# A decode-attention kernel's last projection: two half-width strips, five weight loads, and an unevenly dealt last load

## The chip, the cores and the metric

The kernel runs on one core of one Trainium2 chip. The metric is the device time of one execution in microseconds (us), as the median of several runs. The time of a run is about 2 us longer than the span of its profile (before: 1331.99 for the profiled run, span 1329.9). Times inside an execution are us from the start of the profile's span.

In the views, PE is the matrix engine, PEld its weight loads, DVE the vector engine, ACT the scalar engine and SPq the queue of the sync engine. SBUF is the on-chip memory, and PSUM the one in which matmuls add up. A column strip is a part of PE's columns on which a matmul is placed. A load is split over up to 16 DMA queues (the traces record 16 landings for a load of 128 rows), and its landing is the moment at which one of them, or the last, reports its share as done. The traces don't name the queue of a packet or of a landing. The PE clock is the share of the full clock that was granted.

## The reference

Two attention layers decode one token each. A has 32 heads over 32768 keys. B has 32 query heads over 8 key heads and looks at the last 4096 keys only. Each ends with a projection of its 4096 values to 512.

```python
def _A_ref(x, k_cache, v_cache, wq, wo):            # B: same, with 8 kv heads and a window of 4096 keys
    q = (x @ wq).reshape(B, Sq, H, Dh).transpose(0, 2, 1, 3)
    p = softmax(einsum("bhqd,bhkd->bhqk", q, k_cache) * Dh ** -0.5)
    o = einsum("bhqk,bhkd->bhqd", p, v_cache)
    return o.transpose(0, 2, 1, 3).reshape(B, Sq, H * Dh) @ wo      # wo: 4096 x 512
out = concatenate([a, b], axis=-1)                                  # 1 x 1 x 1024
```

## The kernel before

The kernel streams 570 MB of keys, values and weights through SBUF. A's weights `wo` come last. They lie in SBUF as 128 rows of 32 blocks; a block is 128 x 512 values (128 KB), and one matmul per block adds its part to one PSUM row of 512. The four loads are all issued long ahead, on one queue of the sync engine, and each has a semaphore of its own.

```python
WO_CUTS = {"A": (0, 12, 22, 28, 32), "B": (0, 16, 32)}

def load_wo(self, name, part):
    a0, a1 = self.WO_CUTS[name][part:part + 2]
    src = self.X[name]["wo"].rearrange("(p a) c -> p (a c)", a=32)
    ...
    self.load(self.kbuf[:, off + 512 * a0:off + 512 * a1], src[:, 512 * a0:512 * a1],
              self.wosem[name][part], self.free["k"][t])

def proj_part(self, name, part, out):
    ...
        for a in range(a0, a1):
            row, pos, begin, end = out(a)
            inst = e.matmul(row, lhsT=oz[:, a:a + 1], rhs=wo[:, 512 * a:512 * a + 512], start=begin, stop=end,
                            tile_position=pos, skip_group_check=True)
    return self.op("pe", mm, (self.wosem[name][part], 16), self.c[name]["ozop"])

def store(self, name, bank, off, dep):
    o = self.op("dve", lambda v: v.tensor_copy(self.out_sb[0:1, off:off + 512], bank[0:1, :]), dep)
    self.op("sp", lambda e: e.dma_start(self.out[0, :, off:off + 512], self.out_sb[0:1, off:off + 512])
            .then_inc(self.outsem[name], 16), o)

def emit_proj(self):
    ...                                          # B's 32 matmuls, in four column strips; copy to pb
    for part in range(len(self.WO_CUTS["A"]) - 1):
        last = self.proj_part("A", part, lambda a: (self.PT[0:1, :], None, a == 0, a == 31))
        if part == 0:
            o = ...                              # the matmul that sums B's four strips
            self.store("B", self.ACC, 512, o)
    self.store("A", self.PT, 0, last)
```

## Time and profile before

Part 2 of the page of the kernel before, the two DMA lines: the share in which the 16 DMA engines are busy, in tenths, and GB/s, in 40 slices of the span.

```profile
DMA  9999999999999999999999999999999999999997
GB/s 391 432 432 435 437 428 432 436 438 430 432 434 434 436 432 434 430 440 432 434 430 440 432 432 430 442 430 434 430 440 432 432 432 440 432 432 432 433 435 306
```

The loads bind everywhere but in the last slice. So only the end can change. The chain of waits of the kernel before, its last pieces: start, length, and what the kernel waited for.

```profile
1289.88 28.05 DMA kbuf<-in_A_wo_dram
1317.93 0.04 issue
1317.98 4.41 PE psPT L649 x12
1322.39 0.89 PE psACC L667 x2
1323.27 4.33 PE psPT L649 x20
...
1327.63 0.68 DVE out_sb L655
```

PE waits for A's first 12 blocks, and then it is PE that takes the time: 9.6 us of matmuls, although the last weights land at 1324.09. The view of waits of the kernel before (us in total, times, longest) says the same: one wait for A's weights.

```profile
PEld psPT L649 <- DMA kbuf<-in_A_wo_dram: 3.2, 1, 3.2
```

The windows view of the kernel before. Its last three columns are what is needed here: granted PE clock, share in which the DMA engines are busy, GB/s.

```profile
core 0: us, PE busy (x) PEld busy (x) DVE busy (x) ACT busy (x) POOL busy (x), PEclk, DMA share, GB/s
1318.00:1320.00 2.00, 2.00 (x7) 0.65 (x8) 0.00 (x0) 0.00 (x0) 0.00 (x0) 0.73 0.99 401
1320.00:1321.00 1.00, 1.00 (x4) 0.36 (x3) 0.00 (x0) 0.00 (x0) 0.00 (x0) 0.50 0.75 307
```

PE has half its clock in part of this time. Between 1320 and 1321 a quarter of the DMA engines' time is idle, since some have finished; those that work move 307 / (0.75 x 16) = 25.6 GB/s each.

The trace also records when each of the 16 queues of a load reports its share as landed. For A's last load in the kernel before:

```
1320.77 1320.87 1320.90 1321.01 1321.11 1321.48 1321.48 1321.90 1322.07 1322.10 1322.24 1322.24 | 1323.75 1323.97 1324.05 1324.09
```

Twelve queues finish 1.5 to 3.3 us ahead of the last four. The trace has twelve instruction fetches of 16 KB, 1.0 to 1.1 us each. After the one at 1318.06 a fourth queue joined three late ones, set back by 1.2 to 1.6 (which of the four it is isn't recorded); and four are late in the landings of each of the three loads that follow. What made the other three late isn't shown.

### The profile page before, as it was taken

How to read it: one execution, taken by the hardware profiler on the slowest of the kernel's cores; microseconds unless marked ns; L12 is line 12 of the kernel's file. 1: busy time of each engine (PE TensorE's matmuls, PEld its weight loads, DVE VectorE, ACT ScalarE, POOL GpSimd, SP SyncE). 2: the span in 40 equal slices, each digit the busy share in tenths (PEclk: the TensorE clock that was granted, in tenths of full speed). 3: DMA queues.
4: the chain of work that ended last, by engine and by line, in shares of the span. 5: the costliest groups of instructions: out<-in, count | busy, mean ns of one | idle time of the engine just before them, and what ended most of it. 6: DMA issues, size and time to landing. Idle time of an engine off the chain costs nothing.

```text
span 1329.9 us, 28729 instructions
## 1 busy us (share of the span) xinstructions
PE 970.0 (73%) x13402; PEld 682.1 (51%) x13402; DVE 751.7 (57%) x1345; ACT 54.8 (4%) x167; POOL 2.3 (0%) x17
## 2 busy tenths in 40 slices
PE   3756678687677878767787876778777776877786
PEld 3544456554445655444465544446554444655552
DVE  3654466655556666554566655456665545666562
ACT  0000000000000000000000000000000000000000
POOL 0000000000000000000000000000000000000000
PEclk9767898878879887887988788798878779888888
DMA  9999999999999999999999999999999999999997
GB/s 391 432 432 435 437 428 432 436 438 430 432 434 434 436 432 434 430 440 432 434 430 440 432 432 430 442 430 434 430 440 432 432 432 440 432 432 432 433 435 306
DMA packets 12931, 570.66 MB, mean 429 GB/s; under 512 B 1522, under 2 KB 1524, under 8 KB 1780
## 3 DMA queue, kind: packets, MB, share of 16 engines
q1 hardware_dynamic: 12628, 570.43, 99.3%
q8 instruction: 12, 0.20, 0.1%
q10 hardware_dynamic: 288, 0.00, 0.0%
q14 instruction: 3, 0.02, 0.0%
HBM read 570.43 MB, written 0.00 MB: 429 GB/s over the span
## 4 chain that ended last, share of the span: by engine, by line
DMA 69%; PE 28%; DVE 2%; issue 0%; ACT 0%; SPq 0%
DMA kbuf<-in_A_k_cache_dram 64%; PE psT L491 24%; PE psS L513 4%; DMA kbuf<-in_B_k_cache_dram 3%; DMA kbuf<-in_A_wo_dram 2%; DVE kt L494 1%; PE psPT L649 1%; PE psACC L593 0%; SPq L286 0%; DVE oc_A L609 0%; PE psACC L667 0%; PE psPT L565 0%; ACT psb L541 0%; DVE tr_in L530 0%; DVE out_sb L655 0%
## 5 line engine op out<-in xcount | busy, mean ns | idle before, releaser
L494 DVE COPY kt<-psT 128x1024 bf16<-128x1024 bf16 x1056 | 656.5, 685 | 245.4 <-PE psT L491 243.8
L491 PE MATMUL psT<-ident,kbuf 128*128 128x128 bf16 x8448 | 582.9, 235 | 174.1 <-DMA kbuf<-in_A_k_cache_dram 162.1
L491 PEld LDWEIGHTS psT<-ident,kbuf 128*128 128x128 bf16 x8448 | 543.5, 107 | 266.5 <-DMA kbuf<-in_A_k_cache_dram 170.2
L593 PE MATMUL psACC<-vbuf,ptsb 128*4 128x512 bf16 (+1 forms) x2112 | 181.0, 517 | 22.8 <-ACT ptsb L568 22.0
L513 PE MATMUL psS<-kt,qw 128*32 128x512 bf16 x2048 | 157.6, 385 | 15.5 <-DVE kt L494 15.5
L607 DVE TENSOR_SCALAR oc_A<-psACC,hot_A 128x128 f32<-128x128 f32 x32 | 11.2, 351 | 245.0 <-PE psG L620 245.0
L593 PEld LDWEIGHTS psACC<-vbuf,ptsb 128*4 128x4 bf16 (+1 forms) x2112 | 58.6, 109 | 135.3 <-issue 84.9
L541 ACT ACTIVATE psb<-psS,nb_A 128x512 bf16<-128x512 f32 x32 | 22.0, 687 | 1170.0 <-DVE nb_A L540 1170.0
L513 PEld LDWEIGHTS psS<-kt,qw 128*32 128x32 bf16 x2048 | 34.0, 95 | 58.0 <-DVE kt L494 31.4
L620 PE MATMUL psG<-oc_A,hw 128*32 128x128 f32 (+1 forms) x128 | 19.3, 227 | 52.3 <-DVE oc_A L609 52.3
L620 PEld LDWEIGHTS psG<-oc_A,hw 128*32 128x32 f32 x128 | 11.4, 109 | 62.5 <-DVE oc_A L609 55.0
L565 PE MATMUL psPT<-ident,psb 128*128 128x128 bf16 x136 | 17.4, 268 | 34.0 <-ACT psb L541 34.0
L609 DVE SCALAR_TENSOR_TENSOR oc_A<-psACC,hot_A,oc_A 128x128 f32<-128x128 f32 x96 | 33.7, 351 | 3.4
L530 DVE TENSOR_REDUCE tr_in<-psS 128x1 f32<-128x512 f32 x34 | 23.5, 692 | 17.6 <-PE psS L513 17.6
L565 PEld LDWEIGHTS psPT<-ident,psb 128*128 128x128 bf16 x136 | 9.8, 114 | 37.1 <-ACT psb L541 36.7
L534 PE MATMUL psACC<-rows,tr_in 128*1 128x64 f32 x64 | 8.7, 217 | 25.5 <-DVE tr_in L530 25.5
L568 ACT ACTIVATE ptsb<-psPT 128x512 bf16<-128x512 bf16 x34 | 20.3, 597 | 28.9 <-PE psPT L565 28.9
L534 PEld LDWEIGHTS psACC<-rows,tr_in 128*1 128x1 f32 x64 | 2.7, 81 | 35.1 <-DVE tr_in L530 35.1
L538 PE MATMUL psACC<-mr_A,nscale 1*128 1x1 f32 x64 | 12.1, 256 | 9.7 <-DVE mr_A L537 9.7
L538 PEld LDWEIGHTS psACC<-mr_A,nscale 1*128 1x128 f32 x64 | 9.4, 182 | 15.7 <-DVE mr_A L537 15.7
L540 DVE COPY nb_A<-psACC 128x1 f32<-128x1 f32 x32 | 5.1, 158 | 15.0 <-PE psACC L538 15.0
L447 PE MATMUL psACC<-x_B,vbuf 128*128 128x1 bf16 x128 | 3.6, 165 | 13.6 <-DMA x_B<-in_B_x_dram 13.6
(71 smaller groups left out, 83.8 us busy)
## 6 DMA issues: line engine op xcount, KB each, us to landing
kbuf<-in_B_k_cache_dram SPq DMA_DIRECT2D x2, 4096.0 KB, 32.8
vbuf<-in_B_v_cache_dram SPq DMA_DIRECT2D x2, 4096.0 KB, 24.1
kbuf<-in_A_k_cache_dram SPq DMA_DIRECT2D x2, 4096.0 KB, 22.7
vbuf<-in_B_wq_dram SPq DMA_DIRECT2D x1, 4096.0 KB, 12.5
vbuf<-in_A_wq_dram SPq DMA_DIRECT2D x1, 4096.0 KB, 32.7
kbuf<-in_B_wo_dram SPq DMA_DIRECT2D x2, 2048.0 KB, 32.3
kbuf<-in_A_wo_dram SPq DMA_DIRECT2D x1, 1536.0 KB, 28.1
kbuf<-in_A_wo_dram SPq DMA_DIRECT2D x1, 1280.0 KB, 30.8
```

Source lines behind the costliest of these rows:

```text
L491: inst = e.transpose(T[:, 128 * k:128 * k + 128], src[:, DH * k:DH * k + DH], self.ident[:, :])
L494: self.copies.append(self.op("dve", lambda v: v.tensor_copy(KT[:, :], T[:, :]), o, to="pe"))
L513: inst = e.matmul(self.S[32 * c:32 * c + 32, :], lhsT=win, rhs=self.kt[(bb + c // 2) % NKT][:, 512 * (c % 2):512 * (c % 2) + 512], start=b ...
L530: o = dve(lambda v: v.reduce_max(tr["in"][:, 0:1], self.S[:, :], axis=AXX), self.sdone, self.k_pool, to="pe" if name == "A" else None)
L538: o = self.op("pe", lambda e: e.matmul(self.ACC[:, 64:65], lhsT=self.nscale[:, :], rhs=t["mr"][0:1, :], start=True, stop=True, skip_group_ ...
L541: self.sread = self.op("act", lambda s: s.activation(out=self.psb[:, :], in_=self.S[:, :], func=ACTF.Exp, bias=t["nb"][:, k:k + 1], scale= ...
L565: inst = e.transpose(PT[:, 128 * jj:128 * jj + 128], self.psb[:, 128 * jj:128 * jj + 128], self.ident[:, :])
L568: self.ptread = self.op("act", lambda s: s.activation(out=self.ptsb[:, :], in_=PT[:, 0:512], func=ACTF.Copy), self.psread, to="pe")
L593: inst = e.matmul(acc[32 * c:32 * c + rows, 0:512], lhsT=lhsT, rhs=rhs, start=begin, stop=end, tile_position=(0, 32 * c), skip_group_check ...
L609: o = self.op("dve", lambda v, src=src, hot=hot: v.scalar_tensor_tensor(out=oc, in0=src, scalar=hot, in1=oc, op0=ALU.mult, op1=ALU.add), p ...
L620: return self.op("pe", lambda e: e.matmul(self.G[0:32, c0 + c:c0 + c2], lhsT=win, rhs=t["oc"][g % 2][:, c:c2], start=False, stop=True, ski ...
L649: inst = e.matmul(row, lhsT=oz[:, a:a + 1], rhs=wo[:, 512 * a:512 * a + 512], start=begin, stop=end, tile_position=pos, skip_group_check=True)
```

## The change

PE should do a block in half the time, by taking its 512 columns as two matmuls of 256 in two column strips that run at once (in the kernel before, 64 matmuls in column strips took 6.29 us from 1272.51, 98 ns each at a PEclk of 0.57, where one without strips took 427 at 0.50). Five loads with a smaller last one shorten what is left after the last landing. B's strip sum is moved ahead of A's first block. The last load is dealt unevenly, as 120 rows and 8 rows. The author assumed that these go to 15 queues and to 8, so that one queue has nothing to do for it. With two strips the output is in two PSUM partitions, so it is copied as 65 x 256 and stored as two rows.

```diff
-    WO_CUTS = {"A": (0, 12, 22, 28, 32), "B": (0, 16, 32)}
+    WO_CUTS = {"A": (0, 11, 19, 25, 29, 32), "B": (0, 16, 32)}
@@ load_wo
-        self.load(self.kbuf[:, off + 512 * a0:off + 512 * a1], src[:, 512 * a0:512 * a1], self.wosem[name][part],
-                  self.free["k"][t])
+        cuts = (0, 120, 128) if (name, a1) == ("A", 32) else (0, 128)
+        for p, q in zip(cuts, cuts[1:]):
+            self.load(self.kbuf[p:q, off + 512 * a0:off + 512 * a1], src[p:q, 512 * a0:512 * a1],
+                      self.wosem[name][part], self.free["k"][t])
@@ proj_part: waits for 32 instead of 16 on the last part
+    def halves(self, e, bank, lhsT, rhs, begin, end):
+        for i in range(2):
+            inst = e.matmul(bank[64 * i:64 * i + 1, 0:256], lhsT=lhsT, rhs=rhs[:, 256 * i:256 * i + 256], start=begin,
+                            stop=end, tile_position=(0, 64 * i), skip_group_check=True)
+        return inst
@@ store
-        o = self.op("dve", lambda v: v.tensor_copy(self.out_sb[0:1, off:off + 512], bank[0:1, :]), dep)
-        self.op("sp", lambda e: e.dma_start(self.out[0, :, off:off + 512], self.out_sb[0:1, off:off + 512])
-                .then_inc(self.outsem[name], 16), o)
+        c = slice(off // 2, off // 2 + 256)
+        o = self.op("dve", lambda v: v.tensor_copy(self.out_sb[0:65, c], bank[0:65, 0:256]), dep)
+        self.op("sp", lambda e: e.dma_start(self.out[0, :, off:off + 512].rearrange("a (i x) -> (a i) x", i=2),
+                                            self.out_sb[0:65:64, c]).then_inc(self.outsem[name], 16), o)
@@ emit_proj
+        o = self.op("pe", lambda e: self.halves(e, self.ACC, self.e32[:, 0:1], self.pb, True, True), strips, self.accread)
+        self.store("B", self.ACC, 512, o)
         for part in range(len(self.WO_CUTS["A"]) - 1):
-            last = self.proj_part("A", part, lambda a: (self.PT[0:1, :], None, a == 0, a == 31))
-            ... (B's sum and store after part 0)
-        self.store("A", self.PT, 0, last)
+            o = self.proj_part("A", part, lambda e, lhsT, rhs, a: self.halves(e, self.PT, lhsT, rhs, a == 0, a == 31))
+        self.store("A", self.PT, 0, o)
```

More of the change, by code (lines that the diff above doesn't have):

```diff
@@ L246, in alloc @@
         self.pb = sb("pb", [128, 512], F32)
-        self.out_sb = sb("out_sb", [1, 1024], BF16)
+        self.out_sb = sb("out_sb", [128, 512], BF16)
         self.c = {}
@@ L647, in mm @@
             for a in range(a0, a1):
-                row, pos, begin, end = out(a)
-                inst = e.matmul(row, lhsT=oz[:, a:a + 1], rhs=wo[:, 512 * a:512 * a + 512], start=begin, stop=end,
-                                tile_position=pos, skip_group_check=True)
-            return inst
-        return self.op("pe", mm, (self.wosem[name][part], 16), self.c[name]["ozop"])
+                inst = out(e, oz[:, a:a + 1], wo[:, 512 * a:512 * a + 512], a)
+            return inst
+        return self.op("pe", mm, (self.wosem[name][part], 32 if (name, a1) == ("A", 32) else 16), self.c[name]["ozop"])
@@ L659, in emit_proj @@
     def emit_proj(self):
         for part in range(len(self.WO_CUTS["B"]) - 1):
-            o = self.proj_part("B", part, lambda a: (self.S[32 * (a % 4):32 * (a % 4) + 1, :], (0, 32 * (a % 4)), a < 4, a >= 28))
+            o = self.proj_part("B", part, lambda e, lhsT, rhs, a: e.matmul(
+                self.S[32 * (a % 4):32 * (a % 4) + 1, :], lhsT=lhsT, rhs=rhs, start=(a < 4), stop=(a >= 28),
+                tile_position=(0, 32 * (a % 4)), skip_group_check=True))
         strips = self.op("dve", lambda v: v.tensor_copy(self.pb[:, :], self.S[:, :]), o)
+        o = self.op("pe", lambda e: self.halves(e, self.ACC, self.e32[:, 0:1], self.pb, True, True), strips, self.accread)
@@ L664, in emit_proj @@
+        self.store("B", self.ACC, 512, o)
         for part in range(len(self.WO_CUTS["A"]) - 1):
-            last = self.proj_part("A", part, lambda a: (self.PT[0:1, :], None, a == 0, a == 31))
-            if part == 0:
-                o = self.op("pe", lambda e: e.matmul(self.ACC[0:1, :], lhsT=self.e32[:, 0:1], rhs=self.pb[:, :],
-                                                     start=True, stop=True, skip_group_check=True), strips, self.accread)
-                self.store("B", self.ACC, 512, o)
```

## The prediction

> **What bounds the kernel.** DMA. Part 2 of the page shows the DMA engines at 9 tenths or more in 39 of 40 slices at 430 to 440 GB/s, and part 4 gives the chain 69% DMA. The bytes stay the same, so only the end can shrink.
>
> **The end, before** (timeline, chain of waits, landing records of the trace; us from the span's start). The four loads of A's output weights (12, 10, 6, 4 blocks of 128 KB) land at 1317.93, 1321.03, 1322.85, 1324.09. PE starts at 1317.97 and never waits for a load again: the chain is 4.41 PE (12 matmuls), 0.89 PE (the B strip sum among them), 4.33 PE (20 matmuls). 512 columns take 0.427 at the clock granted first, 0.216 from 1323. PE ends at 1327.60, 3.5 us after the last weights have landed. Then DVE copies 1x512 in 0.68, and the span ends 1.58 after DVE (1328.31 to 1329.89).
>
> **What changes.**
> 1. Two column strips of 256. Strips of this kernel do run together: 64 column-tiled matmuls of 512 columns took 6.29, 98 ns each instead of 427 (timeline, psACC). So one block should take 0.21 (slow clock) or 0.11 (full) instead of 0.43 or 0.22. [...] The loads bring one block per 0.31 (10 blocks between landings 3.1 apart), so PE now keeps up even at the slow clock and waits for every load.
> 2. The B strip sum (0.89) goes ahead of A's first block, into a wait of 2.7. It and B's store leave the chain.
> 3. Cuts 11/8/6/4/3: after the last landing three blocks are left, six half matmuls: 0.6 at full clock, 0.9 at the slow one, drain included.
> 4. The output copy has 256 columns. From 0.19 for 32 columns and 0.68 for 512, estimated 0.42, so 0.26 less.
> 5. Uneven dealing. [...] So one engine loses 24 KB (0.94, at 159 ns per 4 KB packet in the trace), eight gain 3 KB (0.12 each). The last load's 16 landings are: twelve at 1320.8 to 1322.2, four at 1323.75, 1323.97, 1324.05, 1324.09. Freeing one of four late engines gains 0.04 at most; a late engine among the eight costs 0.12. I count 0 (-0.1 to +0.15). Lag comes from instruction fetches (16 KB, about 1.05 us each); one at 1318.06 will come some 2 us earlier[...].
>
> **Sum.** Last landing stays at 1324.1; PE ends at 1324.7 to 1325.1 instead of 1327.6 (-2.5 to -2.9); DVE -0.26; store the same, though in two halves. All of it lies on the chain: -2.9 of 1331.45, i.e. 1328.5 us, 0.2%. Range 1326.8 to 1330.3, as the three runs before lie 1.9 apart. Chances: faster by over 2% 0.01, within 2% 0.985, slower by over 2% 0.005.
>
> **Would show it right.** The chain ends: one DMA piece of A's weights up to about 1324, PE psPT of at most 0.9, DVE about 0.4, store. PE waits for A's weights about five times instead of once. The last landing is within 0.2 of 1324.1. B's output copy comes near 1317, not 1323.
>
> **Would make it wrong.** Half strips that don't overlap (gain only 1.5); an instruction fetch that hits an already late engine (1.2 later); only the freed engine being late (up to 0.9 more gain); B's early store delaying loads on its two engines; a slow split store.

The sum came to -2.9 with -2.5 to -2.9 for PE, -0.26 for DVE, and 0 for step 5 and for the store. Step 5 counts from the assumed 15 and 8 queues. Its 24 KB and 3 KB are estimates from the 16 landings and 128 packets of such a load, 8 packets for each queue, with 3072 B in one (packets of the changed kernel). Lag after an instruction fetch is in the trace of the kernel before: the loads that land by 16.2 us spread by at most 0.6 (12.93 to 13.52), while of the load that lands after the first fetch (at 19.07, 1.05 long) 15 shares come by 23.34 and one at 24.72. Why the fetch at 1318.06 would come 2 us earlier was not shown. The two engines of B's store fit the two landings that the trace of the changed kernel has for it (1321.97 and 1322.57).

## More of the kernel before

The store's issue on the sync engine, kernel before (ns: shortest, median, longest of the two stores):

```profile
L656 SPq DMA_DIRECT2D out_dram<-out_sb x2: 248/280/312, 1324.0 to 1328.3; - x2
```

## The result, and the profile after

The changed kernel takes 1330.23 us (1329.98 to 1330.51, 4 runs) against 1331.50 (1329.72 to 1331.66, 4 runs). The ratio is 0.9994, with a 95% interval of 0.9979 to 1.0009. Ratios are the mean time of one kernel's fast runs over that of the other's of the same rounds, so they are not quite the ratio of the medians. The interval includes 1, so these runs alone don't show a gain. The medians differ by 1.27 us where 2.9 was predicted. The spans of the two profiles differ by 1.6 (1329.9 and 1328.3).

The chain of waits of the changed kernel, its last pieces:

```profile
1290.03 34.16 DMA kbuf<-in_A_wo_dram
1324.18 0.04 issue
1324.22 1.67 PE psPT L658 x14
1325.90 0.02 issue
1325.92 0.42 DVE out_sb L664
```

PE no longer trails the loads by 9.6 us. But the DMA piece ends at 1324.18 with the fourth load, not the fifth, and the PE piece behind it is 1.67 instead of 0.9. The timeline of the changed kernel shows what lies inside this piece (start, length, engine, operation; in brackets idle time of the engine before it and what ended it).

```profile
1324.22 0.51 PEld L658 LDWEIGHTS psPT<-kbuf,oz_A 128*1 128x1 bf16 x8 [1.13 <-DMA kbuf<-in_A_wo_dram]
1324.22 1.66 PE L658 MATMUL psPT<-kbuf,oz_A 128*1 128x256 bf16 x14 [0.84 <-DMA kbuf<-in_A_wo_dram]
1325.06 0.31 PEld L658 LDWEIGHTS psPT<-kbuf,oz_A 128*1 128x1 bf16 x6 [0.33 <-DMA kbuf<-in_A_wo_dram]
```

The weight loads wait once more, until 1325.06, for the last load of A's weights: the matmuls of the fourth part were still draining, so the chain counts the gap as PE. The landing records put the last landing at 1325.02. Before, it was 1324.09. From there it is as predicted: PE needs 0.88, DVE 0.42.

The waits view counts the wait on each load now:

```profile
PEld psPT L658 <- DMA kbuf<-in_A_wo_dram: 3.9, 5, 1.5
```

The windows view of the changed kernel, to be held against the same two lines of the kernel before (columns as there):

```profile
1318.00:1320.00 2.00, 2.00 (x22) 1.09 (x20) 0.23 (x1) 0.00 (x0) 0.00 (x0) 0.50 0.95 377
1320.00:1321.00 1.00, 1.00 (x15) 0.63 (x15) 0.00 (x0) 0.00 (x0) 0.00 (x0) 0.61 0.99 246
```

From 1320 to 1321 the DMA engines are busy for 0.99 of the time, more than before, and move less: 246 / (0.99 x 16) = 15.5 GB/s per working queue, where it was 25.6. The packets themselves are longer. These are the packet times in the traces after 1316, in ns (least, median, greatest):

```
packet of     before            changed
4096 B        159 / 159 / 168   159 / 159 / 329
6144 B        234 / 234 / 244   234 / 236 / 644
3072 B        -                 121 / 152 / 255
```

(The one of 644 ns begins just as an instruction fetch ends; the even version below has one of 654 too.) Nearly all slow packets start between 1319.7, when the first queues come to the last load, and 1323.1, and packets of the earlier loads are among them. So the last load slows its neighbours as well as itself.

The end has a second difference. DVE ends at 1326.34 and the span at 1328.33: 1.99, where it was 1.58. The store's issue on the sync engine of the changed kernel takes about twice as long as before:

```profile
L665 SPq DMA_DIRECT2D out_dram<-out_sb x2: 477/538/599, 1318.3 to 1326.4; - x2
```

### The profile page after: what moved, and what is told of

It reads as the page before. It is cut to its first block, busy times and chain, and to the rows that moved or that the text cites. A ratio compares the mean times of both kernels' runs of the same rounds, so it can differ in the third digit from the quotient of the medians.

```text
span 1328.3 us, 28798 instructions
## 1 busy us (share of the span) xinstructions
PE 968.5 (73%) x13436; PEld 680.1 (51%) x13436; DVE 749.7 (56%) x1345; ACT 54.8 (4%) x167; POOL 2.3 (0%) x17
## 4 chain that ended last, share of the span: by engine, by line
DMA 70%; PE 27%; DVE 2%; issue 0%; SPq 0%; ACT 0%
DMA kbuf<-in_A_k_cache_dram 65%; PE psT L494 23%; PE psS L516 4%; DMA kbuf<-in_B_k_cache_dram 3%; DMA kbuf<-in_A_wo_dram 3%; DVE kt L497 1%; PE psACC L596 0%; SPq L286 0%; PE psPT L658 0%; DVE oc_A L612 0%; PE psPT L568 0%; ACT psb L544 0%; DVE tr_in L533 0%; ACT ptsb L571 0%; PE psG L623 0%
## 5 line engine op out<-in xcount | busy, mean ns | idle before, releaser
L596 PE MATMUL psACC<-vbuf,ptsb 128*4 128x512 bf16 (+1 forms) x2112 | 185.4, 527 | 23.2 <-ACT ptsb L571 21.3
L516 PE MATMUL psS<-kt,qw 128*32 128x512 bf16 x2048 | 157.6, 385 | 15.5 <-DVE kt L497 15.5
L540 DVE TENSOR_REDUCE mr_A<-psACC 1x1 f32<-1x64 f32 x32 | 6.8, 212 | 11.7 <-PE psACC L537 11.7
```

Source lines behind the costliest of these rows:

```text
L516: inst = e.matmul(self.S[32 * c:32 * c + 32, :], lhsT=win, rhs=self.kt[(bb + c // 2) % NKT][:, 512 * (c % 2):512 * (c % 2) + 512], start=b ...
L596: inst = e.matmul(acc[32 * c:32 * c + rows, 0:512], lhsT=lhsT, rhs=rhs, start=begin, stop=end, tile_position=(0, 32 * c), skip_group_check ...
```

## The experiments

The theory P (for placement): which rows a load takes together sets how fast packets go. As one load of 128 rows, the last load leaves the packets at their rate (before: 4 KB in 159 ns, 25.6 GB/s per queue); cut into two loads of neighbouring rows, it slows its own packets and those of the other loads in flight (changed: up to 329 ns, 15.5 GB/s). Why it should be so was inference; no trace shows which rows a queue got or where they went. The rivals: B's early store disturbs the loads (S), the cuts do (C), PE's reading does (M), or the unequal shares do (U). One more was not tested: row p of `wo` in DRAM goes to row p of SBUF, so each cut by rows also changes which rows of DRAM are read at once, and no run here separates the two sides.

One summary for all of them. "Per queue" is the GB/s of the window 1320 to 1321 over 16 times its DMA share.

```
run                what it is                                   median   runs from-to       ratio    span     last     per
                                                                                            to before profile  landing  queue
before             -                                            1331.50  1329.72-1331.66    -        1329.9   1324.09  25.6
changed            -                                            1330.23  1329.98-1330.51    0.9994   1328.3   1325.02  15.5
e12_after_again    changed, second trace                        1330.24  1330.09-1330.33    0.9992   1328.2   1324.93  15.9
e1_even            changed, last load even                      1328.96  1328.82-1329.43    0.9983   1327.1   1324.13  25.1
e2_deal_only       before, last load dealt                      1331.42  1330.73-1331.73    1.0000   1328.7   1325.08  16.5
e3_64_64           changed, dealt 64 and 64                     1330.46  1330.00-1330.89    0.9993   1328.6   1325.15  14.8
e4_one_row_store   e1 with a one-row store                      1328.67  1328.26-1328.89    0.9980   1326.4   1323.76  25.0
e5_rows8_spread    e4, last load as 16 loads of 8 spread rows   1330.99  1329.58-1331.34    0.9994   1329.1   1326.22  24.5
e6_rows8_block     e4, last load as 16 loads of 8 next rows     1331.38  1330.54-1331.62    0.9999   1329.6   1326.67  17.5
e7_full_width      e1 without strips, old store                 1330.83  1329.72-1331.59    0.9996   1327.8   1323.73  -
e8_before_again    before                                       1331.47  1331.13-1331.51    1.0000   1329.4   1323.62  -
e9_before_warm     before, ten idle matmuls added               1331.03  1329.86-1331.35    0.9999   1328.7   1323.53  -
e10_fine_cuts      e4, cuts 12/8/6/4/2                          1328.40  1328.05-1328.88    0.9982   1326.2   1323.70  -
e11_four_cuts      e4, cuts 12/10/6/4                           1328.53  1328.27-1329.49    0.9982   1326.8   1324.05  -
```

### The last load dealt evenly

```diff
-        cuts = (0, 120, 128) if (name, a1) == ("A", 32) else (0, 128)
+        cuts = (0, 128)                      # and wait for 16 on every part
```

> The changed kernel with the last load of A's weights dealt as one load of 128 rows. Theory P (row placement): [...] and packets of every load then in flight slow down. So here 4 KB packets are back at 0.159 us, the window 1320 to 1321 moves at least 300 GB/s at a DMA share under 0.85 (changed kernel: 246 GB/s at 0.99), and the last landing falls from 1325.0 to 1323.6 to 1324.1: span 1.0 to 1.3 us shorter than the changed kernel's 1328.3. Rival S (B's early store disturbs the loads), rival C (the cuts into five loads with 3 KB rows), rival M (PE's half-width reading): slow packets stay, last landing about 1325, span about 1328.3.

Windows view and then the chain of the even version:

```profile
1320.00:1321.00 1.00, 0.85 (x16) 0.61 (x16) 0.00 (x0) 0.00 (x0) 0.00 (x0) 1.00 0.86 346
```

```profile
1290.14 33.98 DMA kbuf<-in_A_wo_dram
1324.13 0.04 issue
1324.17 0.51 PE psPT L658 x6
...
1324.71 0.42 DVE out_sb L664
```

The packets are fast again (4 KB: 159 / 159 / 172 ns) and the last landing is back at 1324.13. The time is 1328.96, 1.27 less than the changed kernel's 1330.23 in another set of runs. B's early store, the five cuts and PE's half-width reading are all still there, so S, C and M fall as causes of the slow packets. The 1.27 is not the dealing's landing alone: of the 1.22 between the spans of the two profiles, 0.89 is the last landing, and 0.32 passes between it and DVE's copy, as PE's last piece ran at the full clock here (PEclk 1.00 from 1324 to 1325) and at 0.50 to 0.60 in the changed kernel. The two further profiles with strips and a last load cut in two (64 and 64 rows, and the changed kernel again) have 0.50 to 0.53 there as well; why isn't known.

### The kernel before with only the last load dealt

```diff
+        cuts = (0, 120, 128) if (name, a1) == ("A", 32) else (0, 128)     # in the kernel before
+        for p, q in zip(cuts, cuts[1:]): self.load(rows p:q ...)
```

> The kernel before with nothing but its last load (4 blocks) dealt 120 and 8 rows. Theory P: packets slow down here too, with none of the other edits; last landing 1 us or more later, 1325.0 to 1326.0 instead of 1324.1; but PE still has its backlog of matmuls to 1327.6, so the span stays at 1329.9, within 0.4. Rivals S, C, M: none of their causes is in this kernel, so packets stay fast and the last landing stays within 0.2 of 1324.1.

The windows view, and then the end of the chain:

```profile
1320.00:1321.00 1.00, 1.00 (x4) 0.08 (x1) 0.00 (x0) 0.00 (x0) 0.00 (x0) 1.00 0.85 225
```

```profile
1289.12 34.92 DMA kbuf<-in_A_wo_dram
1324.04 0.04 issue
1324.08 2.33 PE psPT L652 x10
1326.41 0.02 issue
1326.44 0.68 DVE out_sb L658
```

The window has 225 GB/s at a share of 0.85, 4 KB packets of up to 334 ns, and the last landing is at 1325.08. So the dealing alone makes the loads slow. The median stays (1331.42 beside 1331.52). But the reason that was expected, PE's backlog of matmuls, isn't what this profile shows. It fell at a full PE clock (PEclk 1.00 in the window), and PE had no backlog: it waited for each of A's first three loads. The third, itself slowed, landed at 1324.04 (1322.85 in the kernel before), PE ended at 1326.41, and the span is 1328.7, not 1329.9. So at the full clock the dealing seems to cost time here too: none of the five runs is under 1330.73, while four of the nine of the kernel before in the same set are at 1329.83 to 1330.12.

### All queues busy, but 64 and 64 rows

```diff
-        cuts = (0, 120, 128) if ...
+        cuts = (0, 64, 128) if ...
```

> The changed kernel with the last load dealt 64 and 64 rows: all 16 queues get equal bytes, none is freed, none gets more. Theory P: [...] packets are slow again and the last landing is at 1324.8 or later, span as the changed kernel's or longer (1328 to 1329.5). Rival U (the harm is the unequal share: eight queues carry an extra row, and the loads through 15 queues need more): last landing as in the even version, near 1323.9, span near 1327.2.

The windows view:

```profile
1320.00:1321.00 1.00, 1.00 (x16) 0.59 (x16) 0.00 (x0) 0.00 (x0) 0.00 (x0) 1.00 0.96 228
```

Here no queue is freed: 32 landings are recorded for the load, 16 for each half. That none gets more bytes than another is an estimate from these, as 64 rows on 16 queues are four for each. It is as slow as the uneven deal: 4 KB packets of up to 401 ns, last landing 1325.15 (1324.13 in the even version, with the same bytes in one load), 1.5 us longer than the even version in the same set of runs (1330.46 and 1328.96). So U falls. A cut into two loads of neighbouring rows is enough.

### The even version with the output brought to one row

```diff
-        o = self.op("dve", lambda v: v.tensor_copy(self.out_sb[0:65, c], bank[0:65, 0:256]), dep)
-        self.op("sp", ... self.out_sb[0:65:64, c] ...)
+        o = self.op("dve", lambda v: v.tensor_copy(self.out_sb[0:1, off:off + 256], bank[0:1, 0:256]), deps[0])
+        o2 = self.op("act", lambda s: s.activation(out=self.out_sb[0:1, off + 256:off + 512], in_=bank[64:65, 0:256],
+                                                   func=ACTF.Copy), deps[1])
+        self.op("sp", ... self.out_sb[0:1, off:off + 512] ..., o, o2)
```

> The even version with the output brought to one row: DVE copies the first half, ACT the second half to the same partition, and the store is one row of 1 KB as before. Theory: the store of two rows cost 0.4 more than the one of one row (changed kernel: 1.99 from DVE's end to the span's end; before: 1.58), as the issue takes 0.48 to 0.60 instead of 0.25 to 0.31. Here DVE's or ACT's end to the span's end should be 1.55 to 1.65, with copies of 0.42 to 0.5, so the span is 0.3 to 0.45 under the even version's: about 1326.8, 3.1 under the kernel before. Rival: the store's length is chance or set by the queue's state, and the span is as the even version's within 0.1.

The chain of this version, and in a second fence the issue of its stores:

```profile
1290.13 33.63 DMA kbuf<-in_A_wo_dram
1323.76 0.04 issue
1323.81 0.50 PE psPT L658 x5
...
1324.33 0.41 DVE out_sb L663
```

```profile
L666 SPq DMA_DIRECT2D out_dram<-out_sb x2: 248/285/322, 1318.3 to 1324.8; - x2
```

From the end of the copies (1324.75) to the end of the span it is 1.62; in the even version with the two-row store it is 1.98 (1325.13 to 1327.11), and its issue takes 487 to 630 ns. So the store of two rows costs 0.36. The spans differ by 0.7, as the last landing is also 0.37 earlier here, which is scatter; the medians differ by 0.29. This version beats both kernels: 1328.67 against 1331.52, ratio 0.998 (0.9966 to 0.9993).

### Sixteen loads of eight rows, spread or neighbouring

Both move the same bytes in the same number of loads, and the traces record 128 landings after the 16 at the issues, eight for each load. That it is the same eight queues each time was assumption; the traces don't name them. What differs is which rows go together: in one rows r, r+4, ..., r+28 of a quarter, in the other 8 neighbouring rows.

```diff
+        rows = [slice(32 * (i // 4) + i % 4, 32 * (i // 4) + i % 4 + 29, 4) for i in range(16)]    # e5: rows r, r+4, .., r+28
+        rows = [slice(8 * i, 8 * i + 8) for i in range(16)]                                       # e6: 8 neighbours
```

> The version with one-row store, its last load cut into 16 loads of 8 rows, each of rows r, r+4, ..., r+28 of one quarter[...]. [...] Theory P [...]: 3 KB packets at 0.121 us in the median, at most a few slow ones [...]. [...] the last landing falls to 1322.9 to 1323.5, up to 0.9 earlier than 1323.76; span 1325.6 to 1326.5. Rival U (the number of queues and their shares decide): same landings as the next run[...].

> As the run before, but each of the 16 loads takes 8 neighbouring rows: [...] same bytes, same number of loads; only which rows go together differs. Theory P: [...] 3 KB packets take 0.24 to 0.48 us in the median instead of 0.121, and the last landing comes 1.5 us or more after that of the run before (1325 or later); span at least 1 us longer. Rival U: medians and last landings of the two runs within 0.1 us.

The windows of the two, spread rows first:

```profile
1320.00:1321.00 1.00, 0.77 (x14) 0.38 (x10) 0.00 (x0) 0.00 (x0) 0.00 (x0) 1.00 0.82 321
```

```profile
1320.00:1321.00 1.00, 0.70 (x14) 0.34 (x8) 0.00 (x0) 0.00 (x0) 0.00 (x0) 1.00 0.89 249
```

Spread rows: 24.5 GB/s per queue, 3 KB packets at 121 ns in the median. Neighbouring rows: 17.5 GB/s per queue, 141 ns in the median. So which rows go together matters, as P says (with one trace each, and in SBUF and DRAM alike). But the sizes were wrong. The median of the neighbouring rows rose by a sixth only, not to twice or four times. The last landings are 0.45 apart, not 1.5. And the hope for the spread version failed altogether: its last landing came at 1326.22. Two queues (a DMA share of 0.13 from 1323 to 1324, of 16) still moved 3 KB packets of this load up to 1324.46, so late queues are among those that carried it, and giving these more than their share (double, if it was the same eight each time) is the wrong way round. Then, with the data moved, the completions of the many small loads kept trickling in, one per 0.20 us and queue as the author read the landings, for another 1.76 us.

### Without strips

```diff
-        for i in range(2): e.matmul(bank[64 * i:64 * i + 1, 0:256], ..., tile_position=(0, 64 * i))
+        e.matmul(bank[0:1, :], lhsT=lhsT, rhs=rhs[:, 0:512], ...)         # even load, five cuts, one-row store by DVE
```

> The even version with full-width matmuls and the old store: five even loads, the B sum ahead, no strips. A theory about the strips: at the slow clock one block takes 0.427 here, more than the 0.31 in which it arrives, so runs with the slow clock at the end carry a backlog and span 1328.8 to 1330; at the full clock (0.216) PE keeps up and the span is 1327.0 to 1327.5. So the strips buy 1.5 to 2.5 us in slow-clock runs and about 0.3 in others, and the spread of the runs here should be over 1 us against 0.6 with strips. Rival: strips are needed at every clock, and all runs are at 1329 or more.

The end of its chain of waits:

```profile
1318.55 6.92 PE psPT L657 x32
...
1325.49 0.68 DVE out_sb L660
```

The clock was full during A's blocks (PEclk 1.00 from 1318 to 1326), yet PE didn't keep up: B's 32 matmuls before them had taken 3.35 (2.08 in the kernel before, at PEclk 1.00 from 1313 to 1315), the B sum ended at 1318.55, and PE did all 32 blocks without a wait, 0.216 each. It ended 1.74 after the last landing (1323.73); with strips, in the one-row-store version, it is 0.55. The five runs lie at 1329.72 to 1331.59, a mean of 1330.63 against 1329.07 for the even version with strips (on another chip), and scatter by 1.9 instead of 0.6. So the strips work, and the narrower scatter fits a time that depends less on PE's clock.

### The two groups of runs of the kernel before

The runs of the kernel before fall into two groups, for example 1329.76, 1329.77, 1329.80 and then 1331.38 to 1332.81. A second profile of it fell into the slower group again.

> The kernel before, once more. Its runs lie in two groups, spans near 1328.0 and near 1329.6 to 1331.0. Theory: the group is set by the clock that PE is granted when A's first block lands: full clock gives 12 matmuls in 2.6 to 2.8 us and a span near 1328.0, the slow one 5.1 and 1329.6 or more; no other difference of the tail. If this profile falls in the faster group, it shows the first; if in the slower, it repeats the known one. Rival: the groups differ in the landing of the last load by 1.5 us.

The span is 1329.4, the last landing 1323.62, and the chain has 4.17, 1.12 and 4.33 of PE. It repeats the known profile, with its last landing 0.47 earlier; that is the scatter of the landing.

In the next run ten matmuls into an unused bank keep PE busy ahead of A's first block.

```diff
+        def warm(e):
+            for i in range(10):
+                inst = e.matmul(self.T[1][:, :], lhsT=self.ident[:, :], rhs=self.kt[0][:, 0:512], start=True, stop=True, ...)
+        self.op("pe", warm)
```

> The kernel before with ten extra matmuls of 512 columns into an unused bank, between B's projection and A's first block, so that PE doesn't idle there. Theory H (the two groups of runs of the kernel before, spans near 1328.0 and near 1329.5, come from the clock that PE is granted at A's first block): the trace shows full clock from 1318 on, 12 matmuls in 2.6 to 2.8 instead of 5.1, PE ends about 1325.5, and the runs lie near 1328.0 (within 0.4), the slower group is gone; last landing unchanged. Rival: the groups come from the loads (their last landing moves by 1.5 us between runs); then the two groups stay.

Its chain of waits, from B's matmuls (L649 psS) over the added ones (L666) to A's:

```profile
1313.73 1.88 PE psS L649 x16
1315.61 2.91 PE psT L666 x10
1318.52 2.68 PE psPT L649 x12
1321.20 0.86 PE psACC L673 x2
1322.06 4.33 PE psPT L649 x20
```

The 12 matmuls took 2.68, as expected of the full clock. But four of five runs stayed in the slower group or between the two. In this profile B's own matmuls were at half the clock (PEclk 0.50 from 1314 to 1316) and the added ones took 2.91, so A's blocks began at 1318.45, 1.1 after they had landed (1317.37). The run doesn't settle what makes the groups.

### Other cuts

```diff
-    "A": (0, 11, 19, 25, 29, 32)
+    "A": (0, 12, 20, 26, 30, 32)        # e10
+    "A": (0, 12, 22, 28, 32)            # e11: the four cuts of the kernel before
```

> The one-row-store version with cuts 12, 8, 6, 4, 2 instead of 11, 8, 6, 4, 3. After the last landing two blocks are left instead of three: 0.11 us less at full clock, 0.21 at the slow one. Span 0.1 to 0.2 under the one-row-store version's 1326.4 to 1326.8; it may vanish in the scatter of 0.4. If it is longer, smaller last rows of 2 KB cost the load more than PE gains.

> The one-row-store version with the four cuts of the kernel before (12, 10, 6, 4). Four blocks are left after the last landing instead of three: 0.1 us more at full clock, 0.2 at the slow one; the earlier cuts don't matter, as PE keeps up with the arrival. Span 0.05 to 0.25 longer than the one-row-store version's. Rival: five cuts matter by more (PE builds up a backlog on the block of 10), 0.5 us or more.

Both come out at the one-row-store version's time: 1328.40 and 1328.53 against 1328.67, on different chips. The chain's last PE piece is 0.39 (two blocks), 0.50 (three) and 0.61 (four). The differences are as expected and are smaller than the scatter of the last landing. The cuts hardly matter.

### The changed kernel again

> The changed kernel once more, for a second trace of its end. Theory P: packets of 4 KB up to 0.3 us again between 1319.5 and 1323, window 1320 to 1321 near 240 GB/s at a DMA share above 0.85, last landing 1324.7 to 1325.3 (even versions: 1323.6 to 1324.1), store 1.9 to 2.05 from the end of DVE's copy to the end of the span; span 1327.9 to 1328.6. Rival: the late landing of the first trace was chance (an instruction fetch that hit a late queue); then it falls to 1324.1 or less here.

Its chain of waits, and then its windows view:

```profile
1290.88 34.05 DMA kbuf<-in_A_wo_dram
1324.93 0.04 issue
1324.97 0.82 PE psPT L658 x6
1325.80 0.02 issue
1325.82 0.42 DVE out_sb L664
```

```profile
1320.00:1321.00 1.00, 1.00 (x14) 0.68 (x16) 0.00 (x0) 0.00 (x0) 0.00 (x0) 0.67 0.85 216
```

The last landing is at 1324.93, the queues move 15.9 GB/s each, and 1.98 passes from DVE's end to the end of the span. So neither is chance. Here the chain names the last load itself. Against nine runs of the kernel before, the five runs have a ratio of 0.9992.

## Why the prediction was right or wrong

The sum was -2.9; the medians moved by -1.27, and the spans of the profiles by -1.6.

- **The loads bind, and only the end can shrink:** right. The line of tenths is the same in both pages, with 426 to 442 GB/s in every slice between the first and the last.
- **Two strips run at once, and PE waits for every load:** right. PE waits for A's weights five times instead of once, and the version without strips ended 1.74 after the last landing instead of 0.55. Two, three and four blocks after the last landing took 0.39, 0.50 and 0.61 at the full clock, so a block takes 0.11 instead of the 0.216 without strips.
- **The B sum leaves the chain:** right. B's output copy is at 1317.80 instead of 1323.31.
- **What is left after the last landing:** right. 0.88 of PE at the slow clock (predicted 0.9), 0.42 of DVE (0.42).
- **"5. Uneven dealing ... I count 0 (-0.1 to +0.15)":** this step failed. It measured +0.93 (1325.02 instead of 1324.09), and +0.84 in the second trace; against the even version, +0.9 and +0.8. (Last landings scatter: in the eight traces whose last load is one of 128 rows they lie from 1323.53 to 1324.13.) The step counted bytes per queue only. It took for granted that each queue keeps the 25.6 GB/s of the kernel before. Cutting the load at row 120 brought that down to 15.5, for the other loads in flight too; the even version undoes this, the kernel before gets it from the dealing alone, and 64 and 64 rows do it as well. So the cut is shown as the cause. Why such a cut slows the packets was not shown: the rows per queue of the 120-row load were not seen, and the reading from DRAM was not separated. Of the two 8-row runs the direction is as the theory had it (17.5 beside 24.5 GB/s per queue), but not the size.
- **"store the same, though in two halves":** this step failed too. It measured +0.41 (1.99 instead of 1.58), of which the one-row store took 0.36 away. The prediction had named a slow split store as a risk. The number of rows alone doesn't set the issue time, as the issues of the loads of A's weights took 277 to 478 ns in the changed kernel; what in the two-row store costs was not tested.
- With +0.93 and +0.41 the sum of the prediction becomes about -1.6, which is what the profiles show. With both undone, the one-row-store version has about the gain that was predicted for the change: 1331.52 to 1328.67, -2.85. That it comes so close is partly luck: it is -2.65 by means, which take in both groups of runs, and -3.5 between the two profiles, where the last landing is 0.33 earlier and PE's last piece had the full clock.
- **"one at 1318.06 will come some 2 us earlier":** wrong as well. The instruction fetch came at 1317.64, 0.42 earlier, and four queues were late as before.
- **The clock.** The profile on which the prediction rests comes from the slower group of the kernel before. Means take both groups in: 1331.08 before and 1330.21 changed in the last set of runs, -0.87. What makes the groups stays open: the clock at which PE runs the first 12 matmuls is worth 1.5 to 1.7 us (2.68 in the chain of the run with added matmuls, 4.17 and 4.41 in the two profiles of the kernel before), which is the right size, but no profile of the kernel before fell into the faster group, and the run that was to settle it didn't. An estimate from two traces fits the clock: with the start, copy and store of the second profile (1317.49, 0.68, 1.58) and the pieces of PE with the added matmuls (2.68, 0.86, 4.33) the span is 1327.6, and the spans of the faster group are 1327.7 to 1328.2.
- **Whether the queue that was freed was late at all** stays open too. In the trace of the dealing alone, six landings come late. If these are of four late queues, as in the kernel before, at least two of the four took part in both loads, of 120 and of 8 rows.

## What to carry to other kernels

How a load's rows are cut can cost more than the bytes per queue tell. Here loads that were split along columns, with all 128 rows in each part, ran at 25.0 to 25.6 GB/s per queue; with the last of them cut into 120 and 8 or 64 and 64 rows it was 14.8 to 16.5. So if a load like this must be split, try columns first. The cuts into neighbouring rows also slowed the loads beside it (4 KB packets of up to 401 ns instead of 159), and the cut into spread rows, which did so less (24.5 GB/s per queue), lost its time in late queues and completions. To judge such an edit, look not at the busy share of the DMA engines but at GB/s over busy share: here the share rose from 0.75 to 0.99 while the rate fell. And when an edit speeds up the last compute step, follow the result to the end of the store, as the store of two rows cost more (0.36) than the halved copy saved (0.26).
